# A retention and SwiGLU kernel: ticks at other up and down steps, last scores ahead of the copies, and sums given out one down step earlier

## The chip, the core and the metric

The kernel runs on one core of a Trainium2 chip. The metric is the device time of one execution in microseconds (us), the median of several runs. All data are 32-bit floats.

## The reference

```python
# attention: q, k, v are (8, 8, 576, 64)
scores = scale * np.matmul(q, k.transpose(0, 1, 3, 2))
gamma = 1.0 - 2.0 ** (-5.0 - np.arange(H, dtype=np.float32))
Dmat = np.where(rel >= 0, gamma[:, None, None] ** rel[None, :, :], 0.0)
attn = np.matmul(scores * Dmat[None], v)
# bridge: (B,H,S,D) -> (B*S, H*D) = (4608, 512)
x = attn.transpose(0, 2, 1, 3).reshape(B * S, H * D)
g = x @ w_gate                                  # (4608, 1536)
out = (g / (1 + np.exp(-g)) * (x @ w_val)) @ w_out      # (4608, 512)
```

Each head's scores fall off with distance by a factor gamma per position, and only earlier positions count. So the attention can be done in chunks of 64 positions: within a chunk by masked scores, across chunks by a running 64x64 state per head.

## The kernel before

**Ticks.** The attention works on pairs of heads. There are 8 batches of 4 pairs, so 32 units. `tick(t)` (L673) advances three of them at once: unit t-2 gets its outputs (`own_values`, `earlier_values`, L523 and L545), unit t-1 its states and scores (`new_states` L536, `scores` L561), unit t its transposed q and k (`transposes`, L459). The matmuls of a tick are issued together; what other engines have to do for it is put as functions into the list `pieces`, and `go_on` and `part_on` (L728 and L733) take them from there, one at a time, in the steps that follow. What is left over is taken when the next tick begins. For ticks 10 to 21 ("late" in L710, with masks) the pieces are:

- one that copies the even states on ScalarE (`copies`), copies the outputs of unit t-2 from the PSUM tile `outer` to x on ScalarE (`outputs`), and multiplies the scores by their decay on VectorE (`own`, L579);
- a list of three: `pairs`, which multiplies the last chunk's scores (L589) and forms the odd states (L591), `odd` (L596), and `evens` (L601) with the scaling of the next unit's keys and q on ScalarE;
- the transpose of q on VectorE;
- the transpose of k on VectorE, and with it `next_load(t)`, which issues the load of unit t+2.

**Loads.** `load(i)` (L271) issues, on the SP queue, eight transfers of q and k in elements of 128 bytes (L293) and then those of k again and of v. The tile `qk` has two buffers, so the load that the last piece of tick t issues waits until the transposes of unit t have read that buffer.

**The feed-forward part.** Rows of x are cut into a first tile of 512 and four of 1024. The second to fifth tiles (n from 1 to 4) use a fast matrix multiplication scheme with 26 products in place of 32 blocks; the tables `UP` and `DOWN` (L50 and L78) hold for each product the block sums to be formed, the slot of each operand and what is done with the result. The four PSUM banks A, B, C and E take the products in turn. A tile has three quarters of 26 up steps (`up_step`, L966, four matmuls) and then 26 down steps (`down_step`, L1019, six matmuls). In the second tile (n = 1) the weights' sums are formed as well: each up step stores its weight operand to DRAM on ScalarE's queue (L986). From then on operands are read back: `fetch` (L875) issues the read of the next one on the SP queue into a ring of eight slots. A down step first forms the sums of left operands it is named for (`hops`, L1021), on VectorE or, where its number leaves 1 when divided by 3 and the sum isn't a negated one, on GpSimd. Then come its matmuls, a fetch, the reading of its bank (`reads`, L906), now and then sums of the next tile's x (`x_sums`, L934), and up to three pieces (`go_on(3)`). An up step takes at most one piece, and none in steps 17 and 18 of a quarter, where much is read (L1016).

In the last quarter of the second tile's up steps, step 21 issues three fetches of down operands, step 22 two and step 25 three (L995); the first of them is the operand of the first down step.

**The order of the work** is written out by hand: every queue runs its instructions in the order in which the program issues them. `merge` (L1056) spreads ticks evenly among the steps of a tile. For n = 1 the first quarter runs without ticks; ticks 12 to 17 are spread over the other 52 up steps, which puts them ahead of number 0, 9, 17, 26, 35 and 43 of these; ticks 18 to 21 stand ahead of down steps 2, 7, 13 and 19 (L1156). The ticks of the later tiles are spread evenly.

Of the kernel before, what the change touches and what calls it, by code (L numbers as in the profile page):

```python
# [17 lines left out]
ALU = mybir.AluOpType  # L18
# [136 lines left out]
def kernel(  # L155
# [32 lines left out]
    nc = tc.nc  # L188
# [386 lines left out]
    def masked(i):  # L575
        p, sr, (ret, ret_last, state) = i % HP, last_scores(i), places(i)

        def own():
            nc.vector.tensor_tensor(out=ret, in0=sc, in1=near[:, 2 * p : 2 * p + 2].unsqueeze(2).to_broadcast([P, 2, NFULL, L]),  # L579
                                    op=ALU.mult)  # L580

        def copies():
            (nc.vector.tensor_copy if vector(i + 1) else nc.scalar.copy)(out=even, in_=z[:, 0])

        odd_states = state[:, 1:].rearrange("p (c r) d -> p c r d", r=2)[:, :, 1]

        def pairs():

            nc.vector.tensor_tensor(out=ret_last, in0=sr, in1=last_near[:, p], op=ALU.mult)  # L589
            at = odd_states  # L590
            nc.vector.scalar_tensor_tensor(out=at, in0=even, scalar=step[:, p : p + 1], in1=z[:, 1], op0=ALU.mult, op1=ALU.add)  # L591

        def odd():
            at = odd_states
            for c in range(1, NFULL):
                nc.vector.scalar_tensor_tensor(out=at[:, c], in0=at[:, c - 1], scalar=step[:, HP + p : HP + p + 1],  # L596
                                               in1=at[:, c], op0=ALU.mult, op1=ALU.add)

        def evens():
            at = state[:, 0 : NC - 1].rearrange("p (c r) d -> p c r d", r=2)  # L600
            nc.vector.scalar_tensor_tensor(out=at[:, :, 1], in0=at[:, :, 0], scalar=step[:, p : p + 1], in1=even,  # L601
                                           op0=ALU.mult, op1=ALU.add)

        return [copies, own, [pairs, odd, evens]]

    def to_x(i):
        b, p = divmod(i, HP)
# [63 lines left out]
    pieces = []  # L671

    def tick(t, lo=HP, hi=NP, spread=False, then=None):  # L673
        go_on(len(pieces))
        if hi == HP:

            if lo <= t - 1 < hi:
                scores(t - 1, True)
                new_states(t - 1)
                pieces.extend(masked(t - 1))  # L680
                go_on(3)
            if lo <= t - 2 < hi:
                own_values(t - 2)
            for f in transposes(t) if lo <= t < hi else ():
                f()
            if t + 1 == HP:
                split(0)
            if lo <= t - 2 < hi:
                earlier_values(t - 2)
                if t == HP:  # L690
                    rounding(2)
                    rounding(3)
                to_x(t - 2)[0]()
            if t + 1 == HP:
                rounding(0)
            return
        if lo <= t - 2 < hi:
            own_values(t - 2)
        if lo <= t - 1 < hi:
            new_states(t - 1)  # L700
        if lo <= t - 2 < hi:
            earlier_values(t - 2)
        if lo <= t - 1 < hi:
            scores(t - 1, t - 2 < lo)
        if lo <= t - 1 < hi and whole(t - 2) and not whole(t - 1):
            decay(slice(0, H), slice(0, H), half[1])
        copies, *masks = masked(t - 1) if lo <= t - 1 < hi else (lambda: None,)
        keys, *new = transposes(t) if lo <= t < hi else (lambda: None,)
        outputs = to_x(t - 2)[0] if lo <= t - 2 < hi else lambda: None
        late = needed(1) - 4 <= t < needed(1) - 2 or light(t - 2)  # L710
        if late and masks:
            own, (pairs, odd, evens) = masks
            pieces.extend([lambda: (copies(), outputs(), own()), [pairs, odd, lambda: (evens(), keys())]])
        elif late:
            pieces.append(lambda: (copies(), outputs(), keys()))
        else:
            pieces.extend([lambda: (copies(), keys()), outputs])
            pieces.extend(masks)
        if then and new:
            pieces.extend(new[:-1])  # L720
            pieces.append(lambda: (new[-1](), then()))
        else:
            pieces.extend(new)
            pieces.extend([then] if then else [])
        if not spread:
            go_on(len(pieces))
# [46 lines left out]
    N = len(up)  # L773

    def add(eng, op, view, to=None):
        dst, srcs = view(int(op[1])) if to is None else to, [view(int(a)) for a in op[2:]]
        if op[0] == "neg":
            eng.tensor_scalar(out=dst, in0=srcs[0], scalar1=-1.0, scalar2=None, op0=ALU.mult)
        elif op[0] == "nad" and eng is nc.vector:
            eng.scalar_tensor_tensor(out=dst, in0=srcs[0], scalar=-1.0, in1=srcs[1], op0=ALU.mult, op1=ALU.subtract)  # L780
        elif op[0] == "nad":
            eng.tensor_tensor(out=dst, in0=srcs[0], in1=srcs[1], op=ALU.add)
            eng.tensor_scalar(out=dst, in0=dst, scalar1=-1.0, scalar2=None, op0=ALU.mult)
        else:
            eng.tensor_tensor(out=dst, in0=srcs[0], in1=srcs[1], op=ALU.add if op[0] == "add" else ALU.subtract)  # L785
# [180 lines left out]
    def up_step(n, qd, i):  # L966
# [49 lines left out]
        if max(len(line[-1]) for line in up[i : i + 2]) < 5:  # L1016
            part_on()

    def down_step(n, i):  # L1019
        label, opens, slot, hops, ops = down[i]  # L1020
        for op in hops:  # L1021
            add(nc.gpsimd if i % 3 == 1 and op[0] != "nad" else nc.vector, op, hid_view)
        w = operand().rearrange("p (q x) -> p q x", q=NQ)
        lhs = hid_view(slot)
        b = bank(label, i == 0)
        for qd in range(NQ):
            for m in range(2):
                nc.tensor.matmul(b[:, m * TB : (m + 1) * TB], lhs[:, qd, ts(m, P)], w[:, qd],  # L1028
                                 start=(opens and qd == 0 and m == 0), stop=(qd == NQ - 1), skip_group_check=True)
        fetch()  # L1030

        def result(o, src, negative, vector):
            if negative:
                nc.scalar.mul(out=src, in_=src, mul=-1.0)
            d, t = divmod(o, 4)
            rows = starts[n] + t * TB
            nc.sync.dma_start(out=out[rows : rows + TB, d * TB : (d + 1) * TB].rearrange("(m p) d -> p m d", p=P),
                              in_=src.rearrange("p (m d) -> p m d", m=2))

        if n + 1 == NTILE and i + 1 == N:  # L1040
            _, o, a = ops.pop()
            d, t = divmod(int(o), 4)
            at, rows = part[int(a)], starts[n] + t * TB
            assert ops == [["add", a, "b", a]]
            for m, queue in enumerate((nc.sync, nc.scalar)):
                nc.vector.tensor_tensor(out=at[:, ts(m, TB)], in0=b[:, ts(m, TB)], in1=at[:, ts(m, TB)], op=ALU.add)
                queue.dma_start(out=out[rows + m * P : rows + (m + 1) * P, d * TB : (d + 1) * TB], in_=at[:, ts(m, TB)])
            return
        reads(ops, b, False, result)
        at = 2 * (i - (N - 1 - X_FIRST // 2))  # L1050
        if 0 <= at < X_FIRST and n + 1 < NTILE:
            x_sums(n + 1, at, at + 2, True)
        go_on(3)
# [85 lines left out]
    for n in range(1, NTILE):  # L1139
        upto = needed(n + 1) if n + 1 < NTILE else done  # L1140
        cut = (done + upto + (n == 1) * 2) // 2
        ups = [lambda qd=qd, i=i: up_step(n, qd, i) for qd in range(NQ) for i in range(N)]
        if n == 1:

            for i in range(N):
                ups.pop(0)()
                if i in (6, 14):
                    wait = nc.sync.nop()
                    tc.add_manual_dep(wait.ins, stepped[-1].ins.name,
                                      mybir.DependencyInfo(mybir.DependencyClass.Sync, mybir.DependencyReason.DATA), reason="loads in turn")  # L1150
                    load(FIRST + i // 14)
        downs = [lambda i=i: down_step(n, i) for i in range(N)]
        merge((0.0, ticks(done, cut)), (0.5, ups))
        if n == 1:

            for i, f in reversed(list(zip((2, 7, 13, 19), ticks(cut, upto), strict=True))):  # L1156
                downs.insert(i, f)
            merge((0.5, downs))
        else:
            merge((0.0, ticks(cut, upto)), (0.5, downs))  # L1160
        done = upto

# [29 lines left out]
```

## Time and profile before

| what | us |
|---|---|
| median of 3 runs (lowest, highest) | 1050.15 (1048.26, 1051.46) |
| the profiled execution | 1046.57 |
| its span, first to last instruction | 1044.8 |
| TensorE (PE) busy in the span | 1025.3 |
| VectorE (DVE) busy | 648.1 |
| GpSimd (POOL) busy | 401.8 |
| ScalarE (ACT) busy | 295.2 |
| an up step of PE, from start to start | 1.73 |
| a down step of PE | 2.59 |
| a tick on PE | 2.26 |

The granted TensorE clock was 0.998 of full speed. A line of a timeline gives start and duration in us, engine, line of the program, operation, what it writes and reads, and how many instructions are merged; in brackets the idle time before and what ended it. A line of waits gives who waited for whom, the total, how often, and the longest. SPq is the queue of transfers that SP issues. All times within the execution count from the start of its span.

### The profile page before, as it was taken

Reading aid. Unit: us, or ns where it says so; the run is one execution under the profiler, and the core shown is the slowest. Engines: PE = TensorE matmul, PEld = TensorE weight load, DVE = VectorE, ACT = ScalarE, POOL = GpSimd, SP = SyncE. Lnnn points to the kernel's source line nnn. Section 1 sums busy time; section 2 is a strip of 40 time slices with the busy share of each in tenths; the row PEclk is TensorE's granted clock in tenths of the full one; section 3 lists DMA queues with packets and bytes.
Section 4 is the critical chain, followed back from the end, with each engine's and each line's share of the span. In section 5 each row is a group of like instructions: output and inputs, shape, how many; then the busy total and the mean of one; then the engine's idle time right before and its main releaser. Section 6 shows DMA issues by size and latency. Waiting matters only on the chain.

```text
span 1044.8 us, 21507 instructions
## 1 busy us (share of the span) xinstructions
PE 1025.3 (98%) x8448; PEld 842.7 (81%) x8448; DVE 648.1 (62%) x1063; ACT 295.2 (28%) x646; POOL 401.8 (38%) x347
## 2 busy tenths in 40 slices
PE   6999999999999999999999999999999999999998
PEld 5444555888887888888888888888888888888887
DVE  5578878677767857655468786425476644344644
ACT  4365423243633322132322102222120022231110
POOL 2002367767566035712223048312250483222505
PEclk9999999999999999999999999999999999999999
DMA  9999868776779788765676776545554565555553
GB/s 249 243 280 265 195 196 278 196 209 181 199 195 249 204 216 245 196 166 156 184 219 150 221 184 222 153 137 155 152 173 144 150 201 151 152 153 160 181 161 100
DMA packets 310380, 199.10 MB, mean 191 GB/s; under 512 B 220168, under 2 KB 254984, under 8 KB 310280
## 3 DMA queue, kind: packets, MB, share of 16 engines
q1 hardware_dynamic: 279000, 161.51, 57.2%
q10 hardware_dynamic: 31280, 36.22, 10.4%
q8 instruction: 67, 1.10, 0.4%
q14 instruction: 33, 0.27, 0.1%
HBM read 157.56 MB, written 40.11 MB: 189 GB/s over the span
## 4 chain that ended last, share of the span: by engine, by line
PE 79%; DVE 2%; issue 1%; ACT 0%; DMA 0%; ACTq 0%; DVEq 0%
PE bankC L982 13%; PE bankE L982 12%; PE bankA L982 12%; PE bankB L982 12%; PE bankA L1028 6%; PE bankB L1028 6%; PE bankC L1028 6%; PE bankE L1028 6%; PE outer L531 1%; PE inner L572 1%; PE outer L558 1%; PE inner L542 1%; DVE rest L919 1%; DVE rest L785 0%; PE outer L566 0%
## 5 line engine op out<-in xcount | busy, mean ns | idle before, releaser
L919 POOL TENSOR_TENSOR rest<-rest 128x512 f32<-128x512 f32 x65 | 91.7, 1416 | 298.4 <-DVE rest L919 276.8
L1003 ACT ACTIVATE io<-rest 128x256 f32<-128x256 f32 x180 | 74.9, 417 | 321.9 <-DVE rest L919 277.2
L982 PE MATMUL bankC<-rest,arena 128*128 128x256 f32 x544 | 129.0, 380 | 0.0
L982 PE MATMUL bankA<-rest,arena 128*128 128x256 f32 x544 | 128.7, 379 | 0.0
L785 POOL TENSOR_TENSOR arena<-arena 128x512 f32<-128x512 f32 (+1 forms) x72 | 111.8, 1565 | 39.9 <-DMA up<-arena 26.5
L982 PE MATMUL bankE<-rest,arena 128*128 128x256 f32 x512 | 121.4, 380 | 1.0 <-DVE rest L919 1.0
L982 PE MATMUL bankB<-rest,arena 128*128 128x256 f32 x512 | 121.2, 379 | 0.0
L1010 POOL TENSOR_TENSOR arena<-rest,io 128x256 f32<-128x256 f32 x72 | 52.1, 729 | 166.7 <-ACT io L1003 166.7
L982 PEld LDWEIGHTS bankA<-rest,arena 128*128 128x128 f32 x544 | 103.2, 190 | 14.5 <-issue 0.5
L982 PEld LDWEIGHTS bankC<-rest,arena 128*128 128x128 f32 x544 | 102.9, 190 | 14.5 <-POOL arena L785 0.3
L982 PEld LDWEIGHTS bankE<-rest,arena 128*128 128x128 f32 x512 | 97.0, 190 | 14.6 <-DVE rest L919 1.4
L982 PEld LDWEIGHTS bankB<-rest,arena 128*128 128x128 f32 x512 | 97.0, 190 | 13.3
L785 POOL TENSOR_TENSOR rest<-rest 128x256 f32<-128x256 f32 (+1 forms) x66 | 67.8, 1048 | 102.0 <-DVE rest L419 62.0
L919 DVE TENSOR_TENSOR rest<-bankB,rest 128x512 f32<-128x512 f32 x72 | 48.9, 687 | 67.4 <-PE bankB L982 49.3
L919 DVE TENSOR_TENSOR rest<-bankC,rest 128x512 f32<-128x512 f32 x72 | 48.8, 685 | 66.5 <-PE bankC L982 45.6
L919 DVE TENSOR_TENSOR rest<-bankA,rest 128x512 f32<-128x512 f32 x72 | 48.8, 686 | 62.9 <-PE bankA L982 45.5
L919 DVE TENSOR_TENSOR rest<-bankE,rest 128x512 f32<-128x512 f32 x71 | 48.1, 686 | 61.8 <-PE bankE L982 46.6
L1006 DVE SCALAR_TENSOR_TENSOR arena<-rest,io 128x256 f32<-128x256 f32 x84 | 57.2, 682 | 11.3 <-ACT io L1003 11.3
L1028 PE MATMUL bankA<-arena 128*128 128x256 f32 x252 | 58.0, 380 | 1.3 <-DVE arena L785 1.3
L1028 PE MATMUL bankB<-arena 128*128 128x256 f32 x252 | 58.5, 381 | 0.0
L1028 PE MATMUL bankC<-arena 128*128 128x256 f32 x252 | 58.1, 380 | 0.0
L1028 PE MATMUL bankE<-arena 128*128 128x256 f32 x252 | 57.9, 379 | 0.0
(189 smaller groups left out, 1624.6 us busy)
## 6 DMA issues: line engine op xcount, KB each, us to landing
arena<-up SPq DMA_DIRECT2D x234, 256.0 KB, 2.7
arena<-dn SPq DMA_DIRECT2D x104, 384.0 KB, 3.4
up<-arena ACTq DMA_DIRECT2D x78, 256.0 KB, 3.0
dn<-rest SPq DMA_DIRECT2D x78, 128.0 KB, 1.8
out_dram<-rest SPq DMA_DIRECT2D x31, 256.0 KB, 5.6
qk<-in_q_dram SPq DMA_DIRECT2D x108, 72.0 KB, 2.8
qk<-in_k_dram SPq DMA_DIRECT2D x108, 72.0 KB, 2.3
rest<-in_moe_w_out_dram ACTq DMA_DIRECT2D x6, 1024.0 KB, 6.4
```

What stands on the lines that cost most here:

```text
L531: m = nc.tensor.matmul(value(i, hl, c), s["v"][rows, at], ret[rows, c % 2 if whole(i) else hl, c // 2], start=start, stop=start, skip_grou ...
L542: nc.tensor.matmul(z[half[hl], r, c], s["kn"][chunk(i, hl, 2 * c + r, i < HP)], s["v"][rows, at], start=True, stop=True, skip_group_check= ...
L558: nc.tensor.matmul(xr[half[hl]] if c + 1 == NC else value(i, hl, c), state[half[hl], c, :], s["qT"][half[hl], column(i, hl, c)], start=Fal ...
L572: nc.tensor.matmul(sc[chunk(i, hl, 2 * c + r)[0], r if whole(i) else hl, c], kT[half[hl], at], qT[half[hl], at], start=True, stop=True, sk ...
L785: eng.tensor_tensor(out=dst, in0=srcs[0], in1=srcs[1], op=ALU.add if op[0] == "add" else ALU.subtract)
L919: eng.tensor_tensor(out=at(op[1]), in0=at(op[2]), in1=at(op[3]), op=ALU.add if op[0] == "add" else ALU.subtract)
L982: m = nc.tensor.matmul(b[:, gv * TB : (gv + 1) * TB], w[:, gv, ts(c, P)], rhs[:, c, :], start=(opens and gv == 0 and c == 0), stop=(c == 1 ...
L1003: nc.scalar.activation(out=s, in_=src[:, 0:TB], func=AF.Silu, scale=-1.0 if negative else 1.0)
L1006: return lambda: nc.vector.scalar_tensor_tensor(out=dst, in0=src[:, TB : 2 * TB], scalar=-1.0, in1=s, op0=ALU.mult, op1=ALU.mult)
L1010: nc.gpsimd.tensor_tensor(out=dst, in0=src[:, TB : 2 * TB], in1=s, op=ALU.mult)
L1028: nc.tensor.matmul(b[:, m * TB : (m + 1) * TB], lhs[:, qd, ts(m, P)], w[:, qd], start=(opens and qd == 0 and m == 0), stop=(qd == NQ - 1), ...
```

## The change

It has three parts.

- The multiplication of the last chunk's scores is taken out of `pairs` into a function `last`. In late ticks it is called right after `own`, and the copies to x come after both. In the other ticks the order of instructions stays.
- In the second tile, ticks 12 to 17 now stand ahead of number 0, 7, 15, 25, 33 and 39 of the 52 up steps, and tick 18 stands ahead of down step 1, not 2. Each tick takes its pieces with it, the load among them.
- In every tile with down steps, the sums of left operands of step i+1 are issued in step i, after the reading of its bank and ahead of the x sums and the pieces. Those of step 0 stay in step 0.

```diff
+        def last():
+            nc.vector.tensor_tensor(out=ret_last, in0=sr, in1=last_near[:, p], op=ALU.mult)
+
         def pairs():
 
-            nc.vector.tensor_tensor(out=ret_last, in0=sr, in1=last_near[:, p], op=ALU.mult)
             at = odd_states
...
-        return [copies, own, [pairs, odd, evens]]
+        return [copies, own, [last, pairs, odd, evens]]
...
         if late and masks:
-            own, (pairs, odd, evens) = masks
-            pieces.extend([lambda: (copies(), outputs(), own()), [pairs, odd, lambda: (evens(), keys())]])
+            own, (last, pairs, odd, evens) = masks
+            pieces.extend([lambda: (copies(), own(), last(), outputs()), [pairs, odd, lambda: (evens(), keys())]])
...
-            pieces.extend(masks)
+            for own, (last, pairs, *rest_of) in [masks] if masks else []:
+                pieces.extend([own, [lambda: (last(), pairs()), *rest_of]])
...
+    def hid_sums(i):
+        for op in down[i][3]:
+            add(nc.gpsimd if i % 3 == 1 and op[0] != "nad" else nc.vector, op, hid_view)
+
     def down_step(n, i):
         label, opens, slot, hops, ops = down[i]
-        for op in hops:
-            add(nc.gpsimd if i % 3 == 1 and op[0] != "nad" else nc.vector, op, hid_view)
+        if i == 0:
+            hid_sums(0)
...
         reads(ops, b, False, result)
+        if i + 1 < N:
+            hid_sums(i + 1)
         at = 2 * (i - (N - 1 - X_FIRST // 2))
...
-        merge((0.0, ticks(done, cut)), (0.5, ups))
         if n == 1:
 
-            for i, f in reversed(list(zip((2, 7, 13, 19), ticks(cut, upto), strict=True))):
+            for i, f in reversed(list(zip((0, 7, 15, 25, 33, 39), ticks(done, cut), strict=True))):
+                ups.insert(i, f)
+            merge((0.5, ups))
+            for i, f in reversed(list(zip((1, 7, 13, 19), ticks(cut, upto), strict=True))):
                 downs.insert(i, f)
             merge((0.5, downs))
         else:
+            merge((0.0, ticks(done, cut)), (0.5, ups))
             merge((0.0, ticks(cut, upto)), (0.5, downs))
```

## The prediction

> **What bounds the kernel now.** I read the page first. Its line of PE's busy tenths and its chain that ended last both give TensorE the span:
>
> ```profile
> PE   6999999999999999999999999999999999999998
> ...
> PE 79%; DVE 2%; issue 1%; ACT 0%; DMA 0%; ACTq 0%; DVEq 0%
> ```
>
> PE is busy for 1025.3 of 1044.8 us, so no edit that leaves the matmuls alone can win more than the idle time it removes. Next I read the waits of PE in the stretch 200 to 450 us, which holds nearly all of the second tile's moved ticks and its down stage; after 450 PE shows no wait long enough to be listed.
>
> ```profile
> PE inner L572 <- issue: 2.3, 1, 2.3
> PE bankA L1028 <- DVE arena L785: 1.3, 1, 1.3
> PE outer L566 <- DVE kT L489: 1.1, 1, 1.1
> ```
>
> These three, 4.76 us together by the windows, are all that the change can reach: 0.45% of the time. The timeline of PE puts them at 332.1 (in the middle of tick 18's scores), 360.7 (down step D11) and 272.6 (scores of tick 15). I count the second tile's up steps from 0 to 77 and its down steps from D0 to D25.
>
> Last I read what feeds D0: the timeline of the SP queue, then of VectorE.
>
> ```profile
> 304.69 2.35 SPq L293 DMA_DIRECT2D qk<-in_q_dram  x4
> 307.74 4.85 SPq L293 DMA_DIRECT2D qk<-in_k_dram  x4
> 312.69 0.45 SPq L298 DMA_DIRECT2D kn<-in_k_dram  x1
> 313.23 0.58 SPq L298 DMA_DIRECT2D v<-in_v_dram  x1
> 313.98 8.77 SPq L880 DMA_DIRECT2D arena<-dn  x5
> 327.78 2.21 SPq L293 DMA_DIRECT2D qk<-in_q_dram  x4
> ```
>
> The reader is to see the order: load(18) ends, then five fetches of down operands, and only then load(19). What holds load(19) until 327.78 is the transpose that frees its qk buffer; the waits of SP name it, and VectorE shows it ending at 327.7:
>
> ```profile
> SPq L293 <- DVE kT L489: 5.0, 1, 5.0
> ```
>
> ```profile
> 326.96 0.76 DVE L489 STREAM_TRANSPOSE kT<-qk 128x576 f32<-128x576 f32 x1
> ```
>
> The first matmuls that use a fetched operand are D0's, in the timeline of PE:
>
> ```profile
> 324.30 2.75 PE L1028 MATMUL bankA<-arena 128*128 128x256 f32 x12
> ```
>
> [...] the fourth k request of load(18) waits 3.0 us for a store to up that ACT issued. [...] so a fetch issued behind a load runs behind that load's packets. The trace agrees: the fetch issued at 313.98 has its first 3,072-byte packet at 316.1, just as the last packets of v end (317.05). [...] That is the wait which the second part turns round: before, VectorE's last-score multiply waits for ScalarE's copies (0.95 us in ticks 18 to 20).
>
> **The change part by part.**
>
> *Sums a step ahead.* D11 needs slot 3, the last of the four sums of D8, which VectorE runs at 358.06, 359.01, 360.00 and 360.99 (0.96 us each). They stand behind tick 19's eight instructions, the first of which waits 3.09 us (350.7 to 353.8) for a ScalarE copy that itself waits for D7's bank. In the changed order the four sums are issued at the end of D7, before tick 19's pieces: they fill that wait and end near 354.7, 6 us before D11 asks. Nothing is added: the same sums at the same durations, and the pieces behind them start 0.9 us later at most (353.8 to 354.7), with tick 20's PE work only at 367.4. Gain 1.35. In the other tiles the sums move past nothing that PE waits for: 0, covered by a PE queue that shows no wait after 450 us; the cost if that cover were gone is one sum, 1 us.
>
> *Last scores ahead of the copies.* VectorE loses up to 0.95 us of waiting in each late tick; ScalarE's four to seven copies now start after two VectorE instructions (0.69 and 0.22 us). Queued behind them on ScalarE are key scalings and bank copies; a bank comes round again after about four steps (4 x 1.73 = 6.9 us), so about 1 us of delay is hidden. Value 0, bounds -0.3 to +0.5.
>
> *Ticks at other steps.* Before, ticks 14 and 17 stand at step 17 of a quarter; steps 17 and 18 give out no pieces, so tick 14's last transpose falls in step 50 and runs 272.85 to 273.6, while tick 15's scores want it at 272.6. Now tick 14 stands two steps earlier, its transpose falls in step 48 and tick 15 comes before step 51. From the rows between: the evens end near 265.9, two reads 1.27, transpose of q 0.77, a read 0.68, two products 0.75, transpose of k 0.77, so about 270 against a need at 267.27 + 3.40 = 270.67. Gain 1.10, with 0.7 us to spare. Tick 17 now follows directly on the step that gives out tick 16's transpose: its end (a read at 298.5, then 0.68 + 0.70) is 299.9 against a need at 299.97. Value 0, bound +1.0.
>
> But each tick also issues a load, and here the SP queue is moved past something. Tick 17's transpose and load(19) go from step 76 to step 72, and the first three fetches are issued in step 73. So load(19), ten transfers, now stands **ahead of the fetch of D0's operand**, and cannot start before that transpose. The order of the built program confirms it: the loads, then dn 0 to dn 7 in one run.
>
> When does it start? Step 72 begins at 313.94 - 1.10 = 312.84. VectorE read its bank at 317.42 before, about 1.7 us behind PE; with the q transpose (0.70) in the place of the own-score multiply (0.60) the read is at 316.4, the transpose starts at 317.0 and ends at 317.8. Bounds: 316.2 (no lag behind PE) and 318.8. From the start of a load to the landing of the fetch behind it, the DMA packets give two examples: load(18) 304.69 to 319.55, 14.9 us with stores of up in between, and load(19) 327.78 to 338.93, 11.15 us nearly without. In the changed place the stores of steps 73 to 77 run beside it, and in the built program three of its last six transfers wait for a completion semaphore that one of those stores raises, so it is nearer the first example. I take 12.7. D0's operand lands at 317.9 + 12.7 = 330.6; D0 is due at 324.30 - 1.10 = 323.20 and so waits 7.4 us. Against before, D0 starts 6.3 us later. Ends: 316.2 + 11.15 = 327.35 (+3.05) and 318.8 + 14.9 = 333.7 (+9.4). D1's fetch is issued directly behind and lands about 1 us later, hidden by D0 and tick 18 (2.59 + 2.26).
>
> The 2.31 us of "issue" at 332 stand inside one group of matmuls with no releaser. Nothing in the change addresses it: bounds 0 and -2.31, value 0.
>
> Sum: +6.3 (D0, tick 15's gain included) - 1.35 = +4.95. The profiled execution took 1046.57 (span 1044.8 and 1.77 around it), so it becomes 1051.5. The median of the runs is 3.58 above that execution; I add the difference to it: 1050.15 + 4.95 = 1055.1.
>
> **The rivals.**
> *A, fetch late, as above:* 1055.1, 60%. For it: the queue is in order, and by the page's last part a dn operand lands 3.4 us after its issue at the median, so D0 in time needs an issue before 320.
> *B, the load in front is short (not slower).* Place: the SP queue between 316 and 326. If VectorE keeps up (316.2) and the ten requests run at their floor (8 x 0.5 + 0.4 + 0.6 = 5.0) with dn 4.5 behind, dn lands at 325.7, D0 starts 1.4 later than before, and the 1.35 at D11 pays for it: 1050.2; if the hiccup goes too, 1047.9. It decides where dn lands within 7.9 us of the transpose. Against it: no load between 252 and 345 us was issued in under 6.6. 22%, one in four of it under 1047.
> *C, a second wait on top.* The fetch at its late end (+9.4), or with tick 17's transpose late by 1.0: 1050.15 + 9.4 - 1.35 + 0.5 = 1058.7. For it: 9.1 us of issue in load(18), under stores. 12%.
> *D, the sums don't free D11, or tick 15 still waits.* Then D11's 1.35 stays, or all from tick 15 on moves by 1.1: 1056.5 or 1056.2. 6%.
>
> **Numbers.** A measurement of this kernel tells about 0.3%, 3.15 us, from no change. Faster by more needs under 1047.0: part of B, 6%. Within: the rest of B and the low end of A, where D0 loses under 4.5, 16 + 8 = 24%. Slower: 70%. The range runs from B's middle to C: 1049.8 to 1059.0.
>
> **What would show it.** Of the profile after: PE's wait at the first L1035 bankA with a DMA as releaser, 5 to 9 us; SP's timeline with load(19) ahead of dn 0; no wait of PE on VectorE sums in the down stage, and none on kT at tick 15. If D0 doesn't wait, the step on the SP queue is wrong and the time falls to about 1047.7 (1050.15 - 1.10 - 1.35). If it waits and D11 does too, the sums were sized wrongly.

## The result and the profile after

| what | before | after |
|---|---|---|
| median of 4 runs of each, us | 1049.2 | 1061.8 |
| lowest, highest | 1046.27, 1051.46 | 1061.08, 1062.5 |
| the profiled execution | 1046.57 | 1061.08 |
| its span | 1044.8 | 1059.4 |
| TensorE (PE) busy in the span | 1025.3 | 1030.0 |

The changed kernel is slower: its time is 1.0122 times that of the kernel before, with a 95% interval of [1.0094, 1.015]. The forecast was 1055.1 with a range up to 1059.0: the sign was right, the size too small. (The median of before was 1050.15 over three runs; a fourth brings it to 1049.2.)

Of the page, the lines for PE's busy tenths and for the chain that ended last. The chain now holds transfers and GpSimd, 1% of the span each:

```profile
PE   6999999999996999999999999999999999999998
...
PE 77%; DVE 2%; DMA 1%; POOL 1%; issue 0%; SPq 0%; ACT 0%; ACTq 0%; DVEq 0%; POOLq 0%
```

The waits of PE in the stretch 200 to 460 us (waiter, whom for, total, times, longest):

```profile
PE bankA L1035 <- DMA arena<-dn: 8.7, 1, 8.7
PE bankB L985 <- DVE rest L922: 2.6, 1, 2.6
PE bankA L985 <- POOL arena L788: 1.9, 2, 1.6
PE bankB L1035 <- issue: 1.0, 1, 1.0
```

All three waits of before are gone, also the "issue" of 2.31. The first new one is the forecast one: D0, the first down step, waits for its fetched operand. The SP queue shows why, and PE what follows:

```profile
326.17 1.95 SPq L293 DMA_DIRECT2D qk<-in_q_dram  x4
328.16 3.95 SPq L293 DMA_DIRECT2D qk<-in_k_dram  x4
332.21 0.56 SPq L298 DMA_DIRECT2D kn<-in_k_dram  x1
332.86 1.15 SPq L298 DMA_DIRECT2D v<-in_v_dram  x1
334.12 20.12 SPq L883 DMA_DIRECT2D arena<-dn  x11
```

```profile
339.80 5.25 PE L1035 MATMUL bankA<-arena 128*128 128x256 f32 x12 [8.68 <-DMA arena<-dn]
```

Load(19) stands ahead of all fetches, and starts when VectorE has transposed k for tick 17:

```profile
325.35 0.75 DVE L489 STREAM_TRANSPOSE kT<-qk 128x576 f32<-128x576 f32 x1
```

But D0 also took 5.25 us for the twelve matmuls that took 2.75 before. The windows of PE tell why. Their columns are the stretch, its length, PE's busy time with the number of matmuls, the granted clock (1.00 is full speed), the DMA share and GB/s. The granted clock was halved, twice in this stretch of the kernel.

```profile
266.70:269.20 2.50, 0.00 (x0) 1.00 0.00 0
269.20:269.70 0.50, 0.47 (x2) 0.92 0.00 0
269.70:273.00 3.30, 3.30 (x10) 0.50 0.21 79
...
334.50:339.80 5.30, 0.00 (x0) 0.50 0.99 286
339.80:344.70 4.90, 4.90 (x12) 0.50 1.00 376
```

So the span of after is put together like this, in us: gone are 1.35 (D11), 1.10 (tick 15) and 2.31 ("issue"), together 4.76. New are 8.68 (D0's wait), 2.50 (D0 at half the clock, 5.25 - 2.75), 2.56 (a wait at up step 49), 1.8 (steps 49 and 50 at half the clock: from start to start 3.23 + 2.10 in place of 1.73 + 1.82), 1.93 (GpSimd sums) and 1.0 ("issue"), together 18.5. The difference, 13.7, is most of the 14.6 by which the span grew. Of the last 0.9, one wait of 0.54 at 164.5 is new; the rest is not accounted for.

### The profile page after: what moved, and what is told of

The parts are those of the page before. It is cut to its first block, busy times and chain, and to the rows that moved or that the text cites. A ratio compares the mean times of both kernels' runs of the same rounds, so it can differ in the third digit from the quotient of the medians.

```text
span 1059.4 us, 21507 instructions
## 1 busy us (share of the span) xinstructions
PE 1030.0 (97%) x8448; PEld 845.4 (80%) x8448; DVE 650.1 (61%) x1063; ACT 295.8 (28%) x646; POOL 402.8 (38%) x347
## 4 chain that ended last, share of the span: by engine, by line
PE 77%; DVE 2%; DMA 1%; POOL 1%; issue 0%; SPq 0%; ACT 0%; ACTq 0%; DVEq 0%; POOLq 0%
PE bankC L985 12%; PE bankA L985 12%; PE bankB L985 12%; PE bankE L985 11%; PE bankA L1035 7%; PE bankB L1035 6%; PE bankE L1035 6%; PE bankC L1035 6%; PE outer L531 1%; PE outer L558 1%; PE inner L572 1%; PE inner L542 1%; DVE rest L922 1%; DMA up<-arena 1%; DMA arena<-dn 1%
## 5 line engine op out<-in xcount | busy, mean ns | idle before, releaser
L788 POOL TENSOR_TENSOR arena<-arena 128x512 f32<-128x512 f32 (+1 forms) x72 | 114.9, 1606 | 42.3 <-DMA up<-arena 30.0
L1035 PE MATMUL bankA<-arena 128*128 128x256 f32 x252 | 60.4, 391 | 8.7 <-DMA arena<-dn 8.7
L1035 PEld LDWEIGHTS bankA<-arena 128*128 128x128 f32 x252 | 49.4, 197 | 16.2 <-DVE arena L783 9.1
```

## The experiments

Where D0 is named, the first down step of the second tile is meant. The kernel before is timed anew beside each group of runs, at 1049.0, 1049.2 and 1050.3. A ratio is a run's time over that of the kernel before from the same group, with its 95% interval in brackets. Up steps are counted from 0 to 77, so step 49 is the one that PE reaches at 269.24 in the changed kernel.

**Load(19) held back.** Everything changed, but the load goes out where the kernel before has it.

```diff
-        tick(t, FIRST, NP, True, lambda: next_load(t))
+        tick(t, FIRST, NP, True, lambda: t == 17 or next_load(t))
...
+            ups.insert(len(ups) - 1, lambda: next_load(17))
```

> The changed kernel with all its parts, but load(19) is issued where the kernel before has it on the SP queue: behind the first five fetches of down operands. Theory 1 (the fetch of the first down operand comes late because load(19) stands ahead of it, and TensorE then restarts at half the clock): the 8.68 us wait at D0 and the 2.45 us that D0 took longer both go, so the time falls by about 11.1, from 1061.8 to about 1050.7. Rival (the fetch is late by the store traffic of the last up steps, wherever the load stands): D0 still waits more than 4 us and the time stays above 1057. What remains above the kernel before, some 1.5 us, is then the wait of 2.56 at up step 49, its half clock (1.7) and the 1.93 on GpSimd, less the 1.35 + 1.10 + 2.31 that were removed.

Measured 1050.36, ratio 1.0014 [0.9999, 1.0029]. Its timeline of PE has D0 without a wait and at full speed:

```profile
331.90 2.75 PE L1035 MATMUL bankA<-arena 128*128 128x256 f32 x12
```

Theory 1 holds: the place of one load on the SP queue is worth 11.4 us (1061.8 - 1050.4), the wait and the slow D0 behind it. The rest of the change as a whole is not told apart from before.

**The parts alone.** First the ticks:

```diff
+            for i, f in reversed(list(zip((0, 7, 15, 25, 33, 39), ticks(done, cut), strict=True))):
...
+            for i, f in reversed(list(zip((1, 7, 13, 19), ticks(cut, upto), strict=True))):
```

> The kernel before with only the ticks moved; scores and sums are in the old order. Theory 1 (the moved ticks make nearly all of the loss): D0 waits 7 to 9 us and takes 5.3 instead of 2.75; D11's wait of 1.35 stays; the time is about 1060 to 1063. If the wait of 2.56 at up step 49 shows here as well, it belongs to the moved ticks; if it doesn't, it belongs to the new order of the last scores. Rival (half of the loss comes from the new order of the last scores): the time is below 1058 and neither the GpSimd waits nor step 49's wait shows.

Measured 1061.7, ratio 1.0122 [1.0085, 1.0159], the same as the whole change. Its waits of PE:

```profile
PE bankA L1028 <- DMA arena<-dn: 7.6, 1, 7.6
PE bankB L982 <- DVE rest L919: 2.6, 1, 2.6
PE bankA L982 <- POOL arena L785: 1.5, 1, 1.5
PE bankA L1028 <- DVE arena L785: 1.3, 1, 1.3
...
```

Step 49's wait and a GpSimd wait are there without the other parts: the ticks make them. D0 took 4.42.

Then the last scores alone:

```diff
-            pieces.extend([lambda: (copies(), outputs(), own()), [pairs, odd, lambda: (evens(), keys())]])
+            pieces.extend([lambda: (copies(), own(), last(), outputs()), [pairs, odd, lambda: (evens(), keys())]])
```

> The kernel before with only the last scores put ahead of the copies to x. Prediction's value: no difference, -0.3 to +0.5 us, about 1049 to 1050. Rival (the scores wait on VectorE behind a bank read, ScalarE stands still behind them for up to 3.2 us, and the negations that GpSimd needs come late): ScalarE waits over 3 us for VectorE at the copies to x in at least one tick, TensorE waits 1 to 3 us for GpSimd sums of the up stage, and the time is 1 to 3 us longer.

Measured 1052.03, ratio 1.0028 [1.001, 1.0046]. Neither theory had the place:

```profile
PE bankA L1031 <- DVE arena L788: 2.2, 1, 2.2
...
PE outer L566 <- DVE kT L489: 1.6, 1, 1.6
PE bankA L1031 <- DVE arena L1012: 0.9, 1, 0.9
```

D11's wait grew from 1.35 to 2.15, because the sums of D8 stand behind tick 19's q transpose, which waits for ScalarE's scaling, which now comes after copies that wait for VectorE. The wait on kT at tick 15 grew from 1.10 to 1.58, and D0 has a new wait of 0.94 for a sum on VectorE. With the "issue" 0.54 shorter, the waits grew by 1.7, less than the 3.0 between the medians; the rest is not explained. No GpSimd wait of over 1 us appears.

Then the sums a step ahead alone:

```diff
         reads(ops, b, False, result)
+        if i + 1 < N:
+            hid_sums(i + 1)
```

> The kernel before with only the sums of the down stage given out a step ahead. Prediction's step: the wait of 1.35 at D11 goes and nothing else changes, so about 1048 against a median before of 1049.2. Rival (the sums push back pieces of ticks 18 to 21 or reads of banks, and a wait appears in their place): D11's wait is gone, but a wait of TensorE on a bank or on scores of 0.5 us or more appears in the down stage, and the time is the same or longer. The stall of 2.31 at 332 should stay under both, as nothing here touches it.

Measured 1047.42, ratio 0.9987 [0.9969, 1.0005]. The wait at D11 is gone from the list and nothing takes its place; the point is on the forecast, but the interval reaches no change.

**The last scores beside the other parts.** The kernel with load(19) held back, with the edit of the last scores taken back:

> The kernel before with the ticks moved and the sums a step ahead, the last scores in the old order, and load(19) held back behind five fetches. Against the same with the last scores ahead, which took 1050.36. Theory (the last scores' order is worth little while the sums are a step ahead): within 1 us of 1050.4. Rival (the new order blocks ScalarE in tick 17 by 3.2 us and makes the GpSimd wait of 1.9): the waits of TensorE on GpSimd in the up stage fall under 0.5 us, and the time is 1.5 to 2 us shorter, 1048.5 to 1049.

Measured 1050.13, against 1050.36 with the scores ahead. And the edits of the scores and of the sums together, ticks unmoved:

> The kernel before with the last scores ahead of the copies and the sums a step ahead, the ticks in their old places. Theory (moved ticks make all of the loss; the last scores cost only through the D11 sums, which the step ahead frees): the waits of 2.15 and 0.9 that the last scores alone left at D11 and D0 go, and the time is that of the sums alone, about 1047.4. Rival (the last scores cost by themselves): 1049.5 or more, with a wait of TensorE of 1 us or more that the sums alone did not have.

Measured 1047.79, ratio 0.9989 [0.9967, 1.0012], against 1047.42 for the sums alone. Once the sums go out a step ahead, the times don't tell the order of the last scores apart from no change: the medians of each pair differ by under 0.4, and the intervals are 3 to 5 us wide. The trace of the last kernel says more:

```profile
PE outer L566 <- DVE kT L489: 2.2, 1, 2.2
...
PE bankA L1035 <- DVE arena L1012: 1.1, 1, 1.1
```

D11's wait went, as expected. D0's wait didn't, against the expectation, and the wait on kT at tick 15 is twice the 1.1 of the sums alone. A wait of about 1 us at D0 for that VectorE sum (L1012) is in all three kernels that have the scores ahead and tick 17 in its old place (0.94, 1.06, and 0.95 with one tick put back, below), and in none of the four that have tick 17 there and the scores in the old order. So in these profiles the order costs TensorE about 1 to 2 us of waits, though the times of this pair don't show it.

As for tick 17 in its new place: ScalarE does stand still for 3.24 us behind the scores, but a GpSimd wait of 1.5 was there without them all the same.

**The clock at D0.** Useless matmuls fill the idle time ahead of D0:

```diff
         b = bank(label, i == 0)
+        for _ in range(34 if n == 1 and i == 0 else 0):
+            nc.tensor.matmul(b[:, 0:TB], lhs[:, 0, ts(0, P)], lhs[:, 0], start=True, stop=True, skip_group_check=True)
```

> The changed kernel with 34 extra matmuls of no use (128x128 by 256, 0.216 us each by the 1.73 us of eight, 7.35 us together) issued just ahead of the first down step: they write that step's own bank, which its first real matmul clears. They need no fetched operand, so they fill the 8.68 us in which TensorE stood idle there. Theory (D0 took 5.25 us and not 2.75 because the idle time halved the granted clock): the clock stays at 1.00 there, D0 takes about 2.75, and the time falls by about 2.4, from 1061.8 to about 1059.4, although more work is done. Rival (the slow D0 is the matmuls waiting for their operand piece by piece, or for the bank): D0 still takes over 4.5 us and the time stays or rises.

Measured 1065.99, a miss of mine in size: each is recorded as two matmuls and takes 0.43 us, so the 34 ran for 14.7 us, longer than the wait had been. D0 behind them took 2.75. With 16:

> The changed kernel with 16 extra matmuls of no use just ahead of the first down step. The run with 34 of them showed that one takes 0.43 us (14.7 together), so that it outlasted the wait; 16 take 6.9 us, less than the 8.68 us of idle time, and leave 1.8 of it. Theory (the idle time halves the clock): the clock stays at 1.00 around D0, D0 takes about 2.75 instead of 5.25, and the time falls by about 2.4 to 1059.4. Rival (the slow D0 has another cause): no change, 1061.8.

Measured 1058.73, ratio 1.0084 [1.0065, 1.0103], 3.1 less than the changed kernel by the medians, 4.0 by the ratios, with more work. The timeline of PE:

```profile
330.96 7.07 PE L1034 MATMUL bankA<-arena 128*128 128x256 f32 x32
339.20 2.86 PE L1037 MATMUL bankA<-arena 128*128 128x256 f32 x12 [1.16 <-DMA arena<-dn]
```

D0 began only 0.6 us sooner than in the changed kernel (339.20 against 339.80), but it ran at full speed: the idle time cost twice, once as waiting (8.68 in the changed kernel) and once, about 2.5 us, as the clock behind it. In this profile step 49 ran at full speed as well (more on that below), so not all of the 3.1 need be D0's.

**Step 49.** In the timeline of VectorE of the changed kernel, the read that PE waited for stands behind the three instructions for the odd states of tick 14, and these lie beside three GpSimd sums, given by the timeline of POOL:

```profile
264.83 3.75 DVE L598 SCALAR_TENSOR_TENSOR state<-state,tab 128x64 f32<-128x64 f32 x3
268.50 0.68 DVE L922 TENSOR_TENSOR rest<-bankB,rest 128x512 f32<-128x512 f32 x1
```

```profile
263.17 4.10 POOL L788 TENSOR_TENSOR arena<-arena 128x512 f32<-128x512 f32 x3
```

In the kernel before, the same three took less than half as long:

```profile
266.17 1.49 DVE L596 SCALAR_TENSOR_TENSOR state<-state,tab 128x64 f32<-128x64 f32 x3
```

The three GpSimd sums are left out in the next kernel:

```diff
-            if i > 1:
+            if i > 1 and (qd, i) not in ((1, 19), (1, 21)):
                 w_sums(qd, i)
...
-            else:
+            elif (qd, lo) != (2, 0):
                 add(eng, op, up_view(qd))
```

> The changed kernel without three of the sums that GpSimd forms for the weights of the last but one quarter (the ones that run at 263.2 to 267.3; the results of that quarter are then not those of the reference). Nothing else changes on any engine. Theory (VectorE's three instructions for the odd states of tick 14 took 3.75 us because each stood still while a GpSimd sum ran, and step 49's wait of 2.56 and the half clock behind it follow from that): the three take about 1 to 1.5 us, the wait at step 49 falls under 0.6, the clock stays up, and the time falls by about 4, from 1061.8 to about 1057.8. Rival (they are slow by themselves, or step 49 waits for the reads ahead of them): the three still take over 3 us, the wait stays, and the time is 1061 to 1062.

Measured 1057.09, ratio 1.0068 [1.0051, 1.0085], 4.7 less than the changed kernel by the medians, 5.7 by the ratios. VectorE:

```profile
265.67 0.92 DVE L598 SCALAR_TENSOR_TENSOR state<-state,tab 128x64 f32<-128x64 f32 x3
```

Step 49's wait is gone from the list and no low clock is found there. The theory holds: the same three instructions take 0.31 us each without GpSimd beside them and 1.25 with it, which is a GpSimd sum's own 1.27 to 1.37. A read of a bank took 0.69 beside one of the sums (at 263.63 in the changed kernel) and 0.68 with GpSimd at rest (at 266.51 here).

**One tick put back.** Only tick 17 returns to its old place:

```diff
-            for i, f in reversed(list(zip((0, 7, 15, 25, 33, 39), ticks(done, cut), strict=True))):
+            for i, f in reversed(list(zip((0, 7, 15, 25, 33, 43), ticks(done, cut), strict=True))):
```

> The changed kernel with only tick 17 put back to where the kernel before has it (ahead of up step number 43 of the 52 instead of 39); the other ticks, the scores and the sums stay changed. On the SP queue load(19) then stands behind five fetches of down operands again. Theory (that one place makes the wait at D0, the half clock there and the GpSimd waits of 1.93, since ScalarE's copies of tick 17 then come behind the negations that GpSimd needs): all three go, -13.1, so about 1048.7, with step 49's wait of 2.56 still there. Rival (the GpSimd waits come from the other moved ticks): one of 1 us or more stays, and the time is about 1050.4, as with load(19) alone held back.

Measured 1051.09, ratio 1.0014 [1.0, 1.0028]. D0's wait for the fetch and the GpSimd waits go, as the theory has it, but its number was 2.4 too low. Two other waits, the last two below, come in their place and make 1.9 of it:

```profile
PE bankB L985 <- DVE rest L922: 2.6, 1, 2.6
PE bankA L1035 <- DVE arena L1012: 0.9, 1, 0.9
PE bankC L1035 <- ACT rest L919: 0.9, 1, 0.9
```

So the GpSimd waits come from tick 17's place. That ScalarE's copies then stand ahead of the negations (L946), which GpSimd needs, is read from the timelines (at 311.60 in the changed kernel GpSimd had waited 4.64 us for one) and was not tried by itself.

**Towards a better version.** The sums a step ahead, and tick 13 and 14 one step earlier than before:

```diff
+            for i, f in reversed(list(zip((0, 8, 16, 26, 35, 43), ticks(done, cut), strict=True))):
```

> The kernel before with the sums a step ahead, and of the ticks only number 13 and 14 moved by one step (ahead of up step number 8 and 16 of the 52 instead of 9 and 17); loads and fetches keep their order on the SP queue. Theory (tick 15's wait of 1.10 comes from tick 14's last transpose standing one step too late): this wait goes and nothing else changes, about 1046.3, or 2.7 below the kernel before. Rival (the odd states of tick 14 now run beside three GpSimd sums and are stretched, as in the changed kernel, from 1.5 to 3.7 us): a read of a bank comes late, TensorE waits for it 1 us or more, and the time is 1047.5 to 1049.

Measured 1047.10, ratio 0.9982 [0.9968, 0.9997]. The rival had it in part: the wait on kT fell from 1.10 to 0.52, and a read came late instead (1.08 at L982), the odd states taking 2.71. Tick 15 one step later instead:

```diff
+            for i, f in reversed(list(zip((0, 9, 17, 27, 35, 43), ticks(done, cut), strict=True))):
```

> The kernel before with the sums a step ahead, and of the ticks only number 15 moved, one step later (ahead of up step number 27 of the 52 instead of 26). Theory (the wait of 1.10 at tick 15 is a transpose 1.1 us too late for it, so one step of 1.73 more covers it, and no piece of tick 14 is moved into GpSimd's three sums): the wait is gone, nothing takes its place, and the time is that of the sums alone less 1.1, about 1046.3 against a median before of 1049.2. Rival (tick 15's pieces, one step later, delay tick 16's scores or a read): another wait of 0.5 us or more, and the time is that of the sums alone, about 1047.4.

Measured 1045.65, ratio 0.9966 [0.9954, 0.9979]: faster than the kernel before by 0.3%, and than the changed one. Of its waits of PE between 200 and 460 us two are left:

```profile
PE inner L572 <- issue: 1.9, 1, 1.9
PE bankA L1032 <- DVE arena L1009: 0.2, 1, 0.2
```

By the ratios it gains 2.2 over the sums alone (0.0021 of 1049) where 1.1 was expected; the intervals of the two overlap, so the gain over the sums alone is not shown by the times.

## Why the prediction was wrong in size

Two things failed. The largest is the step "Gain 1.10, with 0.7 us to spare" at tick 15: moving tick 14 made a wait of 2.56 at step 49 and 1.8 of half clock behind it. And the clock has no term in the sum at all, neither there nor at D0, where it was worth 2.50. One by one:

- *Load(19) ahead of D0's fetch.* Right, by mechanism, place and nearly by size. The wait was forecast as 7.4 and was 8.68, and 7.6 with the ticks alone. From the load's start to D0's start 13.6 us passed (326.17 to 339.80), where I took 12.7. The absolute times were off by about 8 us on both sides of the subtraction: the transpose started at 325.35 and not 317.0, and D0 was due at 331.1 and not 323.2, as PE had lost time at step 49 and to GpSimd before; VectorE follows PE, so both moved together.
- *D0's own duration.* This term was missing from the sum. I wrote "D0 is due" and added only the wait, as though TensorE restarted as it had stopped. It was 2.50, and the run with 16 useless matmuls took 3.1 off, of which part may be step 49's. The profile of after has the clock at 0.50 from 334.47, within this stall of 8.68, to 344.71. I had costed a stall of 7 us by its length alone.
- *Tick 15, "Gain 1.10, with 0.7 us to spare".* This is the step that failed most. It priced the odd states and the reads of tick 14 by the rows of their old place ("the evens end near 265.9 ... so about 270"). In the new place the odd states run beside three GpSimd sums and take 3.75 in place of 1.49, the transpose of k starts at 272.62, and a read comes so late that PE stands 2.56 at step 49, which then runs at half the clock. The wait at tick 15 did vanish, but probably only since step 49 stopped PE first: the transpose ended at 273.39, and without that stop and its half clock the scores would have been due near 276.15 - 2.56 - 1.8 = 271.8 (an estimate from the rows). Leaving out the three sums took off 4.7, and then the transpose ends at 271.39, in time for scores at 272.53. The odd states took 1.25 a piece beside GpSimd's sums, against 0.31 without them; by what mechanism, no run here shows.
- *Tick 17, "Value 0, bound +1.0".* Too low. Its odd states were stretched in the same way (3.85 at 313.07, beside GpSimd sums that ran until 316.84), and GpSimd's sums came late: 1.93 on PE, which go when tick 17 is put back. The bound looked only at the transpose that the tick needs, not at what its copies on ScalarE stand ahead of; that these copies are the reason is read from the timelines alone.
- *Sums a step ahead, -1.35.* Right by the traces: D11's wait is gone in each kernel that has this part. The part alone gives 1.6 by the medians, with an interval that reaches no change.
- *Last scores, value 0, bounds -0.3 to +0.5.* Not told apart from nothing where the sums go out a step ahead (two pairs of runs within 0.4 by the medians), wrong alone: 3.0 by the medians. Of these, 0.8 is D11's longer wait, which the sums' move takes away; it doesn't take away the wait of about 1 us at D0 where tick 17 stands in its old place.
- *"Issue" 2.31, value 0.* At the far end of its bound: it went, a gain that was luck, as I had no reason for it, while 1.0 of "issue" came at D1. It is there, 1.8 to 2.0 long, in all five runs that leave tick 18 ahead of D2, and at tick 18 in none of the seven that move it ahead of D1. (The one with 34 matmuls has 1.7 of it elsewhere, after 460 us.) So it goes with tick 18's place; what it is stays open.

Taken by the terms that it counted, the forecast was near: 8.68 - 1.10 - 1.35 = +6.2 against +4.95. What it put at nothing (2.50 + 2.56 + 1.8 + 1.93 + 1.0 = 9.8, less the 2.31 of "issue" that went) is the rest of the error. Rival C, at 1058.7, came nearest, but by luck: it has a later fetch or a late transpose at tick 17, and not the clock or step 49.

## What to carry to other kernels

If a step of work is moved, price it by what runs beside it in the new place, and not by the row of the old place; here three short instructions of VectorE took 1.25 us each beside GpSimd's sums, and 0.31 without them. Price a stall of TensorE of some 2 us or more twice, once as its length and once, as a risk, as the matmuls behind it at half the clock. In these traces, between 200 and 460 us, the shortest stall with half clock behind it was 2.01 us (tick 18, with tick 14 earlier), and the longest without was 2.56 (step 49, with the ticks alone). And look at what else a moved step issues: here one load put ahead of a fetch on the same queue cost 11.4 us, more than the 4.76 of all three waits that the change could remove.

## What the runs showed of the hardware that was not expected

Whether a short stall halved the clock depended, in these traces, on when it fell. The changes of the clock lie on a grid: in the changed kernel at 269.62, 273.03, 334.47 and 344.71 (each found in windows of 0.5 us, by how far the clock within had fallen). From the first to the last are 75.09 us, 22 times 3.413, and the distances between neighbours are 1, 18 and 3 times that. In the kernel before the clock fell at 26.03 and again at 1043.20, 1017.17 us apart, which is 298 times 3.4133. Each trace's own changes of clock, carried on by 3.413 us, give its grid (in the rows for 16 matmuls, before and sums alone from one near the start, 71 to 91 windows on). Laid over the stalls, with the idle share of the windows that hold them:

| kernel, stall | idle | windows end at | idle share | clock after |
|---|---|---|---|---|
| changed, step 49 | 266.67 to 269.24 | 269.62 | 75% | 0.50 |
| with 34 matmuls, step 49 | 264.24 to 266.80 | 267.35 | 75% | 0.50 |
| tick 14 earlier, tick 18 | 333.82 to 335.83 | 336.04 | 59% | 0.50 |
| ticks alone, step 49 | 269.21 to 271.77 | 270.39, 273.80 | 35%, 40% | 1.00 |
| with 16 matmuls, step 49 | 268.37 to 270.93 | 269.85, 273.26 | 43%, 32% | 1.00 |
| before, tick 18 | 332.06 to 334.37 | 333.23, 336.64 | 34%, 33% | 1.00 |
| sums alone, tick 18 | 332.88 to 334.64 | 333.17, 336.58 | 9%, 43% | 1.00 |
| changed, D0 | 331.12 to 339.80 | 334.47, 337.88, 341.30 | 98%, 100%, 56% | 0.50 after each |
| without three sums, D0 | 328.83 to 336.63 | 330.79, 334.20, 337.61 | 58%, 100%, 71% | 1.00, then 0.50, 0.50 |

In the first seven rows a window over half idle, at 59% to 75%, was followed by half clock for 3.41 us, and one under half, at 9% to 43%, was not. The row of the changed kernel's D0 shows when its matmuls were slow, for 4.9 us: the third window began at half clock and was still 56% idle, and the fourth was at half as well. The last row has the one exception. Step 49's stall is 2.55 or 2.56 in seven of the profiles. In five it lies inside one window and costs some 1.8 more (two of them are in the table; in the other three the idle share is 74 or 75%); in two it is split by a mark and costs no more. The windows of the kernel with the ticks alone, beside those of the changed one above, show such a case:

```profile
269.20:271.80 2.60, 0.05 (x2) 1.00 0.00 0
271.80:273.80 2.00, 2.00 (x9) 1.00 0.00 0
```

The same can be laid over every window from 200 to 460 us of the twelve traces in which changes of the clock were found. Eleven that began at full clock were over half idle, from 58% up, and ten of them were followed by half clock; the exception is the 58% above. None of the windows under half idle was, up to 47%. In the first 30 us, one of 74% in the kernel before was followed by half clock, and one of 56% in the changed kernel was not. Where between 47% and 59% the change comes, and whether the share alone decides it, these traces don't show.

The clock also goes with the scatter between runs of one kernel. Of the 136 runs of the kernel before that were timed beside the experiments, the 58 with a mean granted clock of 0.998 or more have a median of 1048.1, and the 27 with 0.995 or less one of 1051.8; the correlation of time and clock is -0.73. That the phase of the grid decides which run is which was not tested.
